# Re-dealing VectorE work and transposes between the attention and FFN stages of a fused transformer block

## The chip, the core and the metric

The kernel runs on one core of a Trainium2 chip. The metric is device microseconds of one execution. PE is TensorE, DVE is VectorE, ACT is ScalarE; SP issues the DMAs. PSUM is the memory into which the matmuls of this kernel write; a *bank* is one of the buffers in it that the kernel numbers 0 to 7. HBM is the memory outside the core.

Because the effect is below 1%, two measures are used. One is the time of whole runs. The other is read from each profile, and I call it **the stretch**: from the start of the first Q-projection matmul behind the first denominators (group 0 and 1) to the start of the first FFN matmul.

## The reference, cut to what matters

S = 2048 tokens, D = 1024, 32 heads of 32. With phi(t) = t+1 or exp(t), the linear attention is

```
q, k, v = split(layernorm_mod(x) @ wqkv)
pq, pk  = phi(q), phi(k)
kv      = sum over tokens of pk^T v          # per head, 32 x 32
den     = pq . sum(pk)                       # per token and head
x       = x + ga * ((pq @ kv / den) @ wo)
x       = x + gb * FFN(layernorm_mod(x))     # gelu(x@w_gate) * (x@w_up) @ w_down, F = 3584
```

## The kernel before, cut to what matters

The kernel never forms `pq @ kv`. It multiplies `kv` and `wo` first (W2 = kv @ wo, one product for each of 8 groups of 4 heads), scales pq by 1/den, and then multiplies pq by W2, one *output chunk* of 128 tokens at a time. "Q group" below means 512 tokens (4 chunks); there are four, numbered 0 to 3. Each group has 8 Q blocks of 128 columns.

1/den is made per head and token as a small row block, written to HBM and read back 32 times replicated ("rb" loads, 2 MB per Q group, in 8 DMAs), so that it lies on the same partitions as pq. Two rb buffers serve four groups, so the load for group 3 has to wait until the scaling of group 1 is done.

```
def phi(bank, dst, ...):                 # evacuates a Q block from PSUM
    ACT: EB = exp(PS(bank))
    DVE: EB = min(EB, 1) + 1e-6
    DVE: dst = max(PS(bank), 0) + EB     # now the bank is free

def pq_scale(sg, h, gs=((0, 2), (2, 4), (4, 6), (6, 8))):
    for g0, g1 in gs:                    # four DVE instructions, 128 x 512 each
        pq[sg][:, g0:g1, half h] *= RB[sg % 2][:, h, g0:g1]

def w2_pair(g):                          # PE: two matmuls into banks 2 and 3; ACT copies them to W2[g]

def q_next():                            # n counts the last 12 Q blocks, the last 8 are group 3; PSUM bank by turns
    b = (0, 1, 2, 0)[n] if n < 4 else (n + 1) % 2
    q_block(...); phi(b, ...)
# ... cut ...
q_next(); kvacc(15); zcols(); q_next(); den(0); rb_load(0); rb_load(1)
kvbd()                                   # DVE: masks kv out of PSUM, into kvbd
q_next(); q_next()
kvt()                                    # PE: 8 transposes of kvbd; ACT copies them
for u in range(8):                       # "W2 step": a Q block and a W2 product
    q_next()
    w2_pair(u)
    if u in (3, 5): pq_scale(0, (u - 3) // 2)
# ... cut ...
for c in range(12):                      # output chunks; banks 6,7 then 2,3 and 0,1 by turns
    wo_chunk(c)                          # 16 matmuls on PE, then DVE adds PSUM to x
    if c == 0: den(1); rb_load(2)
    if c in (0, 1): pq_scale(1, c)
    if c == 1: rb_load(3)
    if c in (4, 5, 6, 7): pq_scale(2 + (c - 4) // 2, c % 2)
    if c < 4: ln2_a(c)                   # layernorm on ACT, then a DMA transpose into h2
    if c == 9: mod2(0, 2); mod2(2, 2)    # 16 small DVE instructions on h2
# then FFN; chunks 12 to 15 are hooked into its first steps
```

## Time and profile before

| | before |
|---|---|
| time, median of the first 3 runs | 847.55 us (845.94 to 847.57) |
| span of the profiled run | 844.6 us |
| stretch | 67.58 us (179.80 to 247.38) |

The first part of the page gives the busy time of each engine, share of the span and number of instructions:

```profile
PE 835.1 (99%) x4229; PEld 386.9 (46%) x4229; DVE 491.8 (58%) x883; ACT 294.9 (35%) x483; POOL 24.3 (3%) x64
```

PE is the bound, so only a gap on PE is worth anything. The list of waits on PE (line, what it waited for, total us, times, longest) holds all of them:

```profile
PE ps_all L467 <- DMA c<-in_c_dram: 2.2, 1, 2.2
PE ps_all L928 <- DVE xall L935: 2.1, 2, 1.3
PE ps_all L565 <- DMA wmq<-in_w_mod_dram: 1.2, 1, 1.2
PE ps_all L653 <- DVE pq L604: 0.7, 1, 0.7
```

L467 and L565 belong to the start of the program. L928 is the matmul of an output chunk, L935 its add; L653 is the Q projection, L604 the last step of phi. The listed waits leave out the modelled tail of a matmul, about 0.16 us each. The loss is read better from the PE timeline (start, duration, line, count, idle before). A warm 512-column matmul takes 0.216 us from start to start:

```profile
179.80 3.63 PE L653 MATMUL ps_all<-h1T,wq 128*128 128x512 bf16 x16
183.35 1.07 PE L829 MATMUL ps_all<-ident,kvbd 128*128 128x128 bf16 x8
184.26 1.89 PE L653 MATMUL ps_all<-h1T,wq 128*128 128x512 bf16 x8
...
196.78 0.59 PE L837 MATMUL ps_all<-wo,kvt 128*128 128x512 bf16 x2
198.03 1.90 PE L653 MATMUL ps_all<-h1T,wq 128*128 128x512 bf16 x8 [0.65 <-DVE pq L604]
...
206.89 27.80 PE L928 MATMUL ps_all<-w,pq 128*128 128x512 bf16 x128
235.58 3.63 PE L928 MATMUL ps_all<-w,pq 128*128 128x512 bf16 x16 [0.89 <-DVE xall L935]
240.46 7.08 PE L928 MATMUL ps_all<-w,pq 128*128 128x512 bf16 x32 [1.26 <-DVE xall L935]
```

Four gaps: the 8 transposes (L829) take 0.91 us where 0.45 would do; the Q block at 198.03 could have started two matmuls after 196.78, at 197.21; the chunk at 235.58 could have started 128 matmuls after 206.89, at 234.51; the one at 240.46 at 239.03. The DVE timeline shows what stood in front of the instructions that PE waited for (L879 is the scaling, L604 frees a Q bank, L935 frees the banks of a chunk):

```profile
194.42 2.48 DVE L879 TENSOR_TENSOR pq<-pq,rb 128x512 bf16<-128x512 bf16 x4
...
197.28 0.69 DVE L604 SCALAR_TENSOR_TENSOR pq<-ps_all,eb 128x512 bf16<-128x512 f32 x1
...
231.89 2.50 DVE L879 TENSOR_TENSOR pq<-pq,rb 128x512 bf16<-128x512 bf16 x4 [2.35 <-DMA rb<-scr_rd]
234.30 1.22 DVE L935 TENSOR_TENSOR xall<-ps_all,xall 128x1024 bf16<-128x1024 f32 x1
236.78 2.50 DVE L879 TENSOR_TENSOR pq<-pq,rb 128x512 bf16<-128x512 bf16 x4 [1.25 <-DMA rb<-scr_rd]
239.19 2.34 DVE L935 TENSOR_TENSOR xall<-ps_all,xall 128x1024 bf16<-128x1024 f32 x2
```

At 194.42 a burst of four scalings stands before a phi. At 231.89 and 236.78 a burst first waits for its rb load to land and then runs, and the adds wait behind both.

### The profile page before, as it was taken

The page shows a single profiled execution, that of the slowest core. Times are in us where ns is not written, and L with a number is a line of the kernel's source. Part 1 is how long each engine was busy: PE and PEld are TensorE (multiplying, and loading weights), DVE is VectorE, ACT ScalarE, POOL GpSimd, SP SyncE. Part 2 cuts the span into 40 slices and gives each one's busy share as a digit, 9 for nine tenths or more (in the row PEclk, how much of TensorE's full clock was granted, in tenths as well). Part 3 has the DMA queues.
Part 4 walks back from the last instruction along what each step waited for, and adds up shares of the span by engine and source line. Part 5 has one row for each costly group of instructions (what it writes and reads, how often), then busy time and mean ns, then how long its engine had stood idle before and what let it go on. Part 6 is the DMA issues. An engine that isn't in the chain of part 4 may idle for free.

```text
span 844.6 us, 11333 instructions
## 1 busy us (share of the span) xinstructions
PE 835.1 (99%) x4229; PEld 386.9 (46%) x4229; DVE 491.8 (58%) x883; ACT 294.9 (35%) x483; POOL 24.3 (3%) x64
## 2 busy tenths in 40 slices
PE   8999999999989999999999999999999999999998
PEld 4454444444434444444444444444444444444445
DVE  5676767877775555564456665445556635565522
ACT  2343333345504345520344442034544204444300
POOL 2000000000200000010000001000000000000000
PEclk9999999999999999999999999999999999999999
DMA  9991824029957587341455533055553305555000
GB/s 283 355 284 26 262 53 98 14 59 238 197 119 222 157 264 205 100 107 31 126 156 154 156 107 81 26 155 151 150 150 100 75 19 156 151 153 145 7 19 26
DMA packets 181750, 112.70 MB, mean 133 GB/s; under 512 B 33080, under 2 KB 172728, under 8 KB 180672
## 3 DMA queue, kind: packets, MB, share of 16 engines
q1 hardware_dynamic: 181696, 111.98, 48.6%
q8 instruction: 34, 0.56, 0.3%
q14 instruction: 20, 0.16, 0.1%
HBM read 100.67 MB, written 4.47 MB: 124 GB/s over the span
## 4 chain that ended last, share of the span: by engine, by line
PE 92%; DMA 4%; SPq 2%; DVE 1%; issue 0%; ACT 0%; DVEq 0%; ACTq 0%
PE ps_all L1025 23%; PE ps_all L1000 23%; PE ps_all L997 23%; PE ps_all L612 12%; PE ps_all L653 6%; PE ps_all L928 3%; DMA rb<-scr_rd 1%; DMA wmq<-in_w_mod_dram 1%; DMA h2T<-xh 1%; PE ps_all L634 1%; DVE pq L879 1%; DMA scr_rd<-rdc 1%; SPq L443 0%; SPq L438 0%; PE ps_all L584 0%; SPq L868 0%
## 5 line engine op out<-in xcount | busy, mean ns | idle before, releaser
L997 PE MATMUL ps_all<-h2T,wg 128*128 128x512 bf16 x896 | 339.6, 379 | 0.0
L1000 PE MATMUL ps_all<-h2T,wu 128*128 128x512 bf16 x896 | 339.6, 379 | 0.0
L1025 PE MATMUL ps_all<-wd,yT 128*128 128x512 bf16 (+1 forms) x924 | 194.1, 373 | 0.0
L1008 ACT ACTIVATE q<-ps_all 128x512 f32<-128x512 f32 x112 | 66.9, 597 | 233.9 <-PE ps_all L997 233.9
L1025 PEld LDWEIGHTS ps_all<-wd,yT 128*128 128x128 bf16 x924 | 90.4, 98 | 103.3
L1000 PEld LDWEIGHTS ps_all<-h2T,wu 128*128 128x128 bf16 x896 | 87.7, 98 | 105.7
L997 PEld LDWEIGHTS ps_all<-h2T,wg 128*128 128x128 bf16 x896 | 87.7, 98 | 105.7
L1010 DVE SCALAR_TENSOR_TENSOR ww<-q,ps_all 128x512 f32<-128x512 f32 x112 | 77.0, 687 | 92.5 <-ACT guh L1009 92.5
L1013 DVE SCALAR_TENSOR_TENSOR ww<-th,guh 128x512 f32<-128x512 f32 x112 | 77.5, 692 | 77.9 <-ACT th L1012 77.9
L1012 ACT ACTIVATE th<-ww 128x512 f32<-128x512 f32 x112 | 70.5, 629 | 84.3 <-DVE ww L1010 84.3
L1015 DVE TENSOR_TENSOR yT<-ww,ps_all 128x512 bf16<-128x512 f32 x112 | 76.9, 687 | 3.8
L1030 DVE TENSOR_TENSOR ps_all<-ps_all,gbb 128x512 f32<-128x512 f32 (+1 forms) x33 | 22.5, 682 | 94.8 <-PE ps_all L1025 94.8
L1009 ACT ACTIVATE guh<-ps_all 128x512 f32<-128x512 f32 x112 | 66.3, 592 | 0.0
L601 ACT ACTIVATE eb<-ps_all 128x512 f32<-128x512 f32 x64 | 37.5, 601 | 78.5 <-PE ps_all L612 38.8
L653 PE MATMUL ps_all<-h1T,wq 128*128 128x512 bf16 x256 | 58.9, 379 | 0.7 <-DVE pq L604 0.7
L928 PE MATMUL ps_all<-w,pq 128*128 128x512 bf16 x256 | 56.6, 379 | 2.1 <-DVE xall L935 2.1
L612 PE MATMUL ps_all<-wk,h1T 128*128 128x512 bf16 x256 | 58.2, 379 | 0.0
L612 PE MATMUL ps_all<-wv,h1T 128*128 128x512 bf16 x256 | 57.7, 379 | 0.0
L602 DVE TENSOR_SCALAR eb<-eb 128x512 f32<-128x512 f32 x64 | 27.1, 424 | 34.6 <-ACT eb L601 34.2
L928 PEld LDWEIGHTS ps_all<-w,pq 128*128 128x128 bf16 x256 | 24.8, 98 | 32.8 <-DVE xall L935 3.1
L612 PEld LDWEIGHTS ps_all<-wv,h1T 128*128 128x128 bf16 x256 | 24.9, 98 | 29.8 <-DVE eb L602 0.3
L612 PEld LDWEIGHTS ps_all<-wk,h1T 128*128 128x128 bf16 x256 | 24.6, 98 | 29.6 <-DVE h1T L538 1.3
(81 smaller groups left out, 397.6 us busy)
## 6 DMA issues: line engine op xcount, KB each, us to landing
wg<-in_B_w_gate_dram SPq DMA_DIRECT2D x56, 512.0 KB, 3.9
wu<-in_B_w_up_dram SPq DMA_DIRECT2D x56, 512.0 KB, 5.1
wmst<-in_w_mod_dram SPq DMA_DIRECT2D x8, 1024.0 KB, 11.5
rb<-scr_rd SPq DMA_DIRECT2D x32, 256.0 KB, 9.0
wd<-in_B_w_down_dram SPq DMA_DIRECT2D x7, 1024.0 KB, 8.2
wmq<-in_w_mod_dram SPq DMA_DIRECT2D x8, 512.0 KB, 7.6
out_dram<-xall SPq DMA_DIRECT2D x31, 128.0 KB, 1.7
xall<-in_A_x_dram SPq DMA_DIRECT2D x3, 1024.0 KB, 11.7
```

The lines of the kernel that those rows point to most:

```text
L612: o = sch.op(T, lambda e, dc=dc: e.matmul(PS(bank), H1[sg][:, dc, ci * P:(ci + 1) * P], W_[:, dc, jg * 512:(jg + 1) * 512], start=(dc == 0 ...
L653: o = sch.op(T, lambda e, dc=dc: e.matmul(PS(b), WQ[:, dc, qc * P:(qc + 1) * P], H1[sg][:, dc, :], start=(dc == 0), stop=(dc == NDC - 1)), ...
L928: last[half] = sch.op(T, lambda e, g=g, half=half: e.matmul(PS(b0 + half), PQ[sg][:, g, ci * P:(ci + 1) * P], W2[:, g, half * 512:(half + ...
L997: og = sch.op(T, lambda e, dc=dc: e.matmul(PS(bg), WG[slot][:, dc, e_ * P:(e_ + 1) * P], H2[sg][:, dc, :], start=(dc == 0), stop=(dc == ND ...
L1000: ou = sch.op(T, lambda e, dc=dc: e.matmul(PS(bu), WU[slot][:, dc, e_ * P:(e_ + 1) * P], H2[sg][:, dc, :], start=(dc == 0), stop=(dc == ND ...
L1008: sch.op(A, lambda e: e.activation(Q1[j][:, :], PS(bg), ACTF.Square, scale=math.sqrt(GELU_A)), prd=pr(bg), wr=rq, note=f"q1 {fc}")
L1009: ogh = sch.op(A, lambda e: e.activation(GUH[j][:, :], PS(bg), ACTF.Copy, scale=0.5), prd=pr(bg), wr=rg, note=f"gh {fc}")
L1010: sch.op(V, lambda e: e.scalar_tensor_tensor(WW[j][:, :], Q1[j][:, :], 1.0, PS(bg), op0=ALU.add, op1=ALU.mult), rd=rq, prd=pr(bg), wr=rw, ...
L1012: sch.op(A, lambda e: e.activation(TH[j][:, :], WW[j][:, :], ACTF.Tanh, scale=GELU_C), rd=rw, wr=rt, note=f"th {fc}")
L1013: sch.op(V, lambda e: e.scalar_tensor_tensor(WW[j][:, :], TH[j][:, :], 1.0, GUH[j][:, :], op0=ALU.add, op1=ALU.mult), rd=rt + rg, wr=rw, n ...
L1015: sch.op(V, lambda e: e.tensor_tensor(YT[:, fc, :], WW[j][:, :], PS(bu), ALU.mult), rd=rw, prd=pr(bu), wr=r_yt(fc), note=f"yT {fc}")
L1025: o = sch.op(T, lambda e, b=b, fc=fc, c0=c0, c1=c1, n=n: e.matmul(PS(b, 0, n), YT[:, fc, ci * P:(ci + 1) * P], WDT[fc // 4][:, fc % 4, c0:c1],
```

## The change

Its intent: no burst of scalings in front of an instruction that frees PSUM, and no transposes before kvbd is done. Scalings of one Q group half come as two pieces of two instructions, one piece per step; those of group 3 move behind chunks 10 and 11 and the rest behind the last of them; the rb load of group 3 moves with them, behind the four DMA transposes on SP's queue; the KV transposes come one Q block later, so the W2 products lag one step, and the last one gets banks 4 and 5.

```
-        def w2_pair(g):
-            b0 = 2
+        def w2_pair(g, b0=2):
...
-        def pq_scale(sg, h, gs=((0, 2), (2, 4), (4, 6), (6, 8))):
+        GH = [((0, 2), (2, 4)), ((4, 6), (6, 8))]
+
+        def pq_scale(sg, h, gs):
...
-        kvt()
         for u in range(NG):
             q_next()
-            w2_pair(u)
-            if u in (3, 5):
-                pq_scale(0, (u - 3) // 2)
+            if u == 0:
+                kvt()
+            else:
+                w2_pair(u - 1)
+            if u in (2, 3):
+                pq_scale(0, 0, GH[u - 2])
+            if u in (5, 6):
+                pq_scale(0, 1, GH[u - 5])
+        w2_pair(NG - 1, 4)
...                                            # in the loop over chunks c_:
-            if c_ in (0, 1):
-                pq_scale(1, c_)
-            if c_ == 1:
+            if 1 <= c_ <= 8:
+                pq_scale(1 + (c_ - 1) // 4, (c_ - 1) // 2 % 2, GH[(c_ - 1) % 2])
+            if c_ == 4:
                 rb_load(3)
-            if c_ in (4, 5, 6, 7):
-                pq_scale(2 + (c_ - 4) // 2, c_ % 2)
+            if c_ in (10, 11):
+                pq_scale(3, 0, GH[c_ - 10])
...                                            # ahead of the FFN loop:
+        pq_scale(3, 1, GH[0] + GH[1])
```

## The prediction

> **What bounds the kernel.** TensorE. The page's first part has PE busy 835.1 of 844.6 us (99%), granted clock 1.0; the list of waits has four for PE, 6.2 us together, all before 241 us. Warm 512-column matmuls start 0.216 us apart, which agrees with the 215.7 ns of the Trainium skill, "TensorE: Matmul & The Clock Gate", section "Wait — 56ns, not 53.3ns?". From 247 us to the end the chain has no gap, so only gaps in 174 to 247 us, where the change acts, can be won back.
>
> **The gaps there** (PE timeline, start to start, less the matmuls at their pace):
> 1. KV transposes: 8 take 0.91 us where 8 x 0.057 = 0.45 would do; they wait for kvbd on DVE (182.80 to 184.08). Lost 0.46.
> 2. The last Q block starts at 198.03, not 197.21: its PSUM bank waits for the phi of block 5, which on DVE stands behind four scalings (194.42, 2.48 us). Lost 0.82.
> 3. Output chunk 9 starts at 235.58, not 234.50: its banks wait for chunk 7's residual add, behind four scalings that waited for an rb load of Q group 3 (231.89, after 2.35 us idle for DMA). Lost 1.08.
> 4. Chunk 10 starts at 240.46, not 239.03: the same with the last burst (236.78, after 1.25 us idle). Lost 1.43.
> Sum 3.79 us.
>
> **What the change removes, adds, moves.** No instruction is added or removed: the same matmuls, DMA bytes and 32 scalings of about 0.62 us. Bursts of 2.5 us become pieces of 1.25 us. A W2 step on DVE is then 1.1 (phi) + 1.25 = 2.35 us against PE's 2.16, but only in pairs of steps, and two Q banks give slack; a chunk is 1.22 + 1.25 = 2.5 against 3.45. VectorE being strict FIFO (same page, "Architectural detail"), place in its order decides what PE waits for. Transposes after the next Q block find kvbd done. The last W2 pair in other banks need not wait for a 1.0 us copy. The rb load for Q group 3 moves behind all four h2 transposes on the DMA queue: I estimate its halves land about 240 and 245 us, not 232 and 237, but its scalings now stand after chunks 10 and 11, and PE needs them only at chunk 12 (261 us before). The last transpose lands about 235, the h2 modulation runs about 238 to 242, and FFN can start at about 243.6.
>
> **On the critical path:** all four gaps are on PE's own chain. I expect 3.4 to 3.8 us back; perhaps 0.1 to 0.4 lost again at the start of FFN, where chunk 10's add (behind 16 modulations, 4.2 us) ends about when PE wants its bank.
>
> **Predicted:** 847.55 - 3.65 = 843.9 us; 842.3 to 845.9 holds it 8 times in 10 (the runs before spread 1.6 us). Faster by over 2%: 0.003; within 2%: 0.992; slower by over 2%: 0.005.
>
> **Right if the profile shows:** KV transposes in about 0.45 us; no PE wait on a phi at L653; none on the residual add in chunks 9 and 10; the first FFN matmul near 243.7 instead of 247.4, and all after it shifted alike; no DVE idle for rb loads before chunk 9; the last rb load landing later without PE waiting.
>
> **Wrong if:** the later rb load or the last h2 transpose holds DVE so long that the first FFN banks come late (new waits near 243 to 254 us); the W2 stage, now DVE-bound in places, makes Q blocks 6 or 7 wait; or noise hides 0.4%.

(In its point 2, "the last Q block" is a slip: the block at 198.03 is the last but one, and the phi it waits for is that of the block two before it.)

## More of the kernel before

The fourth part of the page, the chain of work that ended last, gives its shares by engine and already says that a DMA is part of it (by the page's list, about 1% each are the rb loads, the transposes into h2, the store of 1/den, and a weight load, wmq, at the start of the program):

```profile
PE 92%; DMA 4%; SPq 2%; DVE 1%; issue 0%; ACT 0%; DVEq 0%; ACTq 0%
```

## The result, and the profile after

| | before | after |
|---|---|---|
| time, median (lowest to highest), 4 runs each | 847.56 us (845.94 to 847.92) | 843.27 us (843.05 to 843.71) |
| span of the profiled run | 844.6 us | 841.3 us |
| stretch | 67.58 us | 64.54 us |

The ratio is 0.9954, 95% interval 0.9937 to 0.9971: a real gain of about 0.5%, inside the 2% that count as "same".

In the page of the kernel after, the first part and the shares of the chain by engine:

```profile
PE 830.7 (99%) x4149; PEld 387.9 (46%) x4229; DVE 492.0 (58%) x883; ACT 294.9 (35%) x483; POOL 24.4 (3%) x64
...
PE 96%; DVE 2%; issue 1%; ACT 1%; DMA 0%; ACTq 0%
```

The 4.4 us less of PE busy time must not be read as saved work. PE did the same 4229 matmuls (the weight loads are all there), but 80 records are missing, so busy time is missing with them. The run "only the chunk stage" below, which has all 4229 records, shows 835.0 us. The second line is a real difference as far as the rb loads, the h2 transposes and the store are gone from the chain; the weight load of the start is gone too, but that varies with the start (it is there again, at 1%, in that run below).

The waits on PE (line numbers moved: L928 became L934) and the PE timeline at the same places:

```profile
PE ps_all L467 <- DMA c<-in_c_dram: 2.2, 1, 2.2
PE ps_all L653 <- DVE pq L604: 0.7, 1, 0.7
PE ps_all L653 <- issue: 0.2, 1, 0.2
PE ps_all L653 <- DVE ve L483: 0.2, 1, 0.2
```

(The two waits of 0.2 us are as long as one matmul, and the run with all 4229 records does not list them; I take them for missing records.)

```profile
179.46 5.35 PE L653 MATMUL ps_all<-h1T,wq 128*128 128x512 bf16 x23
184.65 0.61 PE L829 MATMUL ps_all<-ident,kvbd 128*128 128x128 bf16 x8
185.92 1.90 PE L653 MATMUL ps_all<-h1T,wq 128*128 128x512 bf16 x8 [0.66 <-DVE pq L604]
...
206.00 38.16 PE L934 MATMUL ps_all<-w,pq 128*128 128x512 bf16 x172
244.00 0.38 PE L1003 MATMUL ps_all<-h2T,wg 128*128 128x512 bf16 x1
```

Eleven chunks (176 matmuls, 4 records missing) now run from 206.00 to 244.00 without a gap: 176 x 0.2158 = 37.98 us. The gaps in the chunk stage and before the last Q blocks are gone. On DVE the adds of the chunks now wait for PE and for no load; this is the one of chunk 7, for which chunk 9 waited before:

```profile
230.39 1.23 DVE L941 TENSOR_TENSOR xall<-ps_all,xall 128x1024 bf16<-128x1024 f32 x1 [1.03 <-PE ps_all L934]
```

But the KV transposes did not simply lose their wait. They now take their 0.45 us, and the Q block behind them starts at 185.92 instead of 184.65 + 0.45 = 185.10: a gap of 0.82 us that the kernel before did not have, in place of 0.46. The DVE timeline shows what that block waits for:

```profile
182.45 1.29 DVE L823 TENSOR_TENSOR kvbd<-ps_all,bmask 128x384 bf16<-128x384 f32 x3
...
184.72 0.42 DVE L602 TENSOR_SCALAR eb<-eb 128x512 f32<-128x512 f32 x1
185.17 0.69 DVE L604 SCALAR_TENSOR_TENSOR pq<-ps_all,eb 128x512 bf16<-128x512 f32 x1
```

The block needs bank 0. Its last user was the Q block two before it, whose phi stands on DVE behind kvbd and another phi, and ends at 185.86 (185.17 + 0.69).

The sum of the gaps explains the stretch: before, 0.46 + 0.82 + 1.07 + 1.43 = 3.78 us; after, 0.82. The difference, 2.96, is close to the 3.04 by which the stretch got shorter.

### The profile page after: what moved, and what is told of

Its sections match the earlier page's. It is cut to its first block, busy times and chain, and to the rows that moved or that the text cites. A ratio compares the mean times of both kernels' runs of the same rounds, so it can differ in the third digit from the quotient of the medians.

```text
span 841.3 us, 11255 instructions
## 1 busy us (share of the span) xinstructions
PE 830.7 (99%) x4149; PEld 387.9 (46%) x4229; DVE 492.0 (58%) x883; ACT 294.9 (35%) x483; POOL 24.4 (3%) x64
## 4 chain that ended last, share of the span: by engine, by line
PE 96%; DVE 2%; issue 1%; ACT 1%; DMA 0%; ACTq 0%
PE ps_all L1006 23%; PE ps_all L1031 23%; PE ps_all L1003 22%; PE ps_all L612 12%; PE ps_all L934 7%; PE ps_all L653 6%; PE ps_all L668 1%; PE ps_all L634 1%; DVE h1T L538 1%; PE ps_all L584 0%; PE ps_all L836 0%; PE ps_all L565 0%; PE ps_all L519 0%; DVE ww L1019 0%; DVE ww L1016 0%
## 5 line engine op out<-in xcount | busy, mean ns | idle before, releaser
L1003 PE MATMUL ps_all<-h2T,wg 128*128 128x512 bf16 x859 | 325.6, 379 | 0.0
L653 PE MATMUL ps_all<-h1T,wq 128*128 128x512 bf16 x245 | 56.8, 379 | 1.4 <-DVE pq L604 0.7
L934 PE MATMUL ps_all<-w,pq 128*128 128x512 bf16 x251 | 56.0, 379 | 0.3
L934 PEld LDWEIGHTS ps_all<-w,pq 128*128 128x128 bf16 x256 | 25.0, 98 | 30.2 <-issue 0.2
```

What stands on the lines that cost most here:

```text
L653: o = sch.op(T, lambda e, dc=dc: e.matmul(PS(b), WQ[:, dc, qc * P:(qc + 1) * P], H1[sg][:, dc, :], start=(dc == 0), stop=(dc == NDC - 1)), ...
L934: last[half] = sch.op(T, lambda e, g=g, half=half: e.matmul(PS(b0 + half), PQ[sg][:, g, ci * P:(ci + 1) * P], W2[:, g, half * 512:(half + ...
L1003: og = sch.op(T, lambda e, dc=dc: e.matmul(PS(bg), WG[slot][:, dc, e_ * P:(e_ + 1) * P], H2[sg][:, dc, :], start=(dc == 0), stop=(dc == ND ...
```

## The experiments

**Theory A.** In DVE's fixed order, an instruction that frees a PSUM bank waits for everything ahead of it. The two gaps of the chunk stage come from scalings that stand ahead of an add before their rb load has landed, and the time of the landing is set by the DMA queue, so time won earlier on PE is lost there again. The gain is therefore almost wholly from moving the scalings of group 3 behind the chunks.
**Rival B** (the sum in my prediction): the four gaps are independent and each is worth its length.
**Rivals E and F**: it is the smaller pieces that help; it is only the place of the scalings, and the order of the rb load and the DMA transposes is of no account.

The stretch was read in each profile:

| kernel | stretch, us | time, us (median) | before, same chip (median) |
|---|---|---|---|
| before / before, again | 67.58 / 67.96 | 847.18 (again) | 846.53 |
| after / after, again | 64.54 / 64.77 | 844.30 (again) | 846.54 |
| only the W2 stage dealt out | 68.52 | 846.80 | 846.53 |
| only the KV transposes moved | 67.74 | 846.99 | 846.53 |
| only the chunk stage dealt out | 65.09 | 843.67 | 846.53 |
| after, KV transposes as before | 64.26 | 843.20 | 846.54 |
| after, last W2 product in banks 2, 3 | 65.95 | 844.52 | 846.54 |
| after, whole bursts in the chunk stage | 64.54 | 843.26 | 846.81 |
| after, whole bursts in the W2 stage | 65.37 | 843.97 | 846.81 |
| after, group 1 scaled early, rb load of group 3 early | 64.54 | 842.90 | 846.81 |
| before, rb load of group 3 late | 78.29 | 856.76 (one run) | 846.81 |
| after, a third PSUM bank for Q blocks | 63.71 | 842.56 | 846.54 |

All gave the right result.

### One part of the change at a time

*Only the W2 stage*: the kernel before with

```
-            if u in (3, 5):
-                pq_scale(0, (u - 3) // 2)
+            if u in (2, 3):
+                pq_scale(0, 0, GH[u - 2])
+            if u in (5, 6):
+                pq_scale(0, 1, GH[u - 5])
```

> The kernel before with only the scaling of Q group 0 dealt in half-group pieces over four W2 steps. Theory A (the gaps of the chunk stage are pinned to the landing of the rb loads of Q group 3, which the DMA queue sets, so what PE wins earlier it waits for there): the 0.8 us wait of a Q block in the W2 stage goes, but chunk 9 and chunk 10 still start within about 0.3 us of where they start before (235.6 and 240.5), their two gaps grow by about 0.8 us together or chunk 9's alone, and the time is within 0.3 us of before. Rival B (the four gaps are independent and add): 0.8 us faster, about 846.7.

Its PE timeline:

```profile
196.51 0.59 PE L837 MATMUL ps_all<-wo,kvt 128*128 128x512 bf16 x2
196.94 1.89 PE L653 MATMUL ps_all<-h1T,wq 128*128 128x512 bf16 x8
...
205.79 28.08 PE L932 MATMUL ps_all<-w,pq 128*128 128x512 bf16 x128
236.23 3.63 PE L932 MATMUL ps_all<-w,pq 128*128 128x512 bf16 x16 [2.36 <-DVE xall L939]
241.12 7.08 PE L932 MATMUL ps_all<-w,pq 128*128 128x512 bf16 x32 [1.26 <-DVE xall L939]
```

The Q block no longer waits (196.94 is two matmuls behind 196.51), and the second denominators are done 1.1 us earlier than before. Yet chunk 9 starts at 236.23: its wait grew from 0.89 to 2.36 us and swallowed all. Rival B falls; the ratio is 1.0004 (0.9992 to 1.0017), and its 0.8 us would be 0.9991. The chunk starts were not within the 0.3 us that I had written, but 0.65 us later than in the first profile of the kernel before; they lie between the two profiles of that kernel (235.58 and 236.37 for chunk 9). Why the time won does not reach the rb load is seen in the chain of this kernel, where the row of 1/den goes to HBM, and the first rb load follows:

```profile
208.58 5.49 DMA scr_rd<-rdc
...
214.08 0.33 SPq L868
```

The same piece of the chain in the kernel before:

```profile
209.57 4.38 DMA scr_rd<-rdc
213.96 0.34 SPq L868
```

The store was issued 1 us earlier and landed at the same time. Ahead of it in the queue stand four weight loads of 512 KB. The Trainium skill, "DMA: Bandwidth & Descriptors", section "Queues, rings and completion order", says that each DMA engine consumes the descriptors of a ring in order; these two landings agree: the DMA engines were busy with the weight loads up to 212 us in both (DMA share 1.15 and 1.20 from 211 to 212, 0.23 and 0.48 from 212 to 213), and the store landed at 213.95 and 214.07. No run moved the weight loads, so this step rests on the traces alone.

*Only the KV transposes* (later by one Q block, W2 one step behind, last product in banks 4 and 5):

> The kernel before with only the KV transposes one Q block later, the W2 products one step behind and the last one in other banks. Theory A: the wait moves from the transposes to the next Q block and grows from about 0.46 to about 0.82 us, because that block's bank still holds the Q block whose phi stands behind the kvbd product on DVE; this loss of about 0.36 us is swallowed by the wait for the rb loads, so the time is within 0.3 us of before. Rival B (my prediction: the transposes' gap goes): 0.46 us faster.

The gap behind the transposes was 0.82 us and no wait was inside them; the stretch, 67.74, lies between those of the two profiles of before, and the ratio is 1.0005 (0.9992 to 1.0017). Rival B, which was my prediction for this part, falls by the trace; the whole runs alone would not exclude its 0.46 us (0.9995). That the loss of 0.36 us was swallowed later is not shown by this run: chunk 9's gap was 0.94 us, less than the 1.07 and 1.42 of the two profiles of before, but these two differ by as much.

*Only the chunk stage* (`GH` and the last two pieces of the diff above, on the kernel before):

> The kernel before with only the scaling of groups 1 to 3 re-dealt over the output chunks and the rb load of group 3 moved behind the transposes. Theory A: no PE wait on the residual add in chunks 9 and 10; the W2 stage keeps its waits of 0.46 and 0.82 us; time about 0.46 us above the kernel after, so about 843.7, 3 to 4 us faster than before: nearly all of the gain is here. Rival B (four gaps add): 2.5 us faster than before, about 845.0.

```profile
206.60 38.16 PE L930 MATMUL ps_all<-w,pq 128*128 128x512 bf16 x176
```

No wait in the chunks, and the 0.82 us of the Q block and the 0.46 of the transposes still there. The stretch is 2.5 us shorter than that of the first profile of before and 2.9 shorter than that of the second; ratio 0.9967 (0.9954 to 0.9979). The stretch of the first profile alone would fit rival B as well; it is the two runs above that decide. With this part alone about four fifths of the gain in the stretch is there (2.49 of 3.04 us), less than the "nearly all" that I had expected; with it in place the W2 part is worth its own 0.83 us (the run with whole bursts in the W2 stage, below), which it was not before.

*The kernel before, again*:

> The kernel before itself, profiled again, to see what varies from run to run. Theory A: the starts of chunks 9 and 10 vary by some tenths of a us with the landing of the rb loads (they were 235.58 and 240.46), and the sum of the two gaps with them, which would explain why its times spread 2 us and those of the kernel after 0.7 us. Rival: the chunk gaps are the same to 0.1 us and the spread comes from the start of the program, before 45 us.

Chunk 9 started at 236.37, not 235.58, and its gap was 1.42, not 1.07 us, while chunk 10's gap was 1.43 both times. The first Q block of the stretch was also 0.42 us later. Both theories hold in part: the start of the program varies, and the landing of the rb loads varies on top of it.

*The kernel after, again*:

> The kernel after itself, profiled again beside its variants. Theory A: gap of 0.82 us behind the KV transposes again, no gap in the chunks, time 843.0 to 843.8; its spread is below 1 us, as only the start of the program varies.

The stretch was 64.77 us with the same gap of 0.82 us, as expected. The 0.23 us above the first profile are two Q blocks that waited 0.1 us each (197.29 and 199.56): DVE had stood 0.41 us at the first scaling of group 0, whose rb load landed late, so the W2 stage has little slack even with the pieces. But the times were not as expected: 842.79 to 845.91 us. The view by windows of this run (stretch of time, length, PE, weight loads, DVE, ACT and POOL busy, granted clock, DMA share, GB/s) shows where:

```profile
20.00:24.00 4.00, 2.71 (x40) 1.60 (x39) 0.90 (x3) 0.00 (x0) 0.00 (x0) 0.93 0.98 305
24.00:28.00 4.00, 4.00 (x18) 1.55 (x17) 0.00 (x0) 0.00 (x0) 0.00 (x0) 0.64 1.01 323
```

In the profiled run the granted clock fell to 0.64 at 24 to 28 us, long before any changed line, and the stretch began at 182.08 instead of 179.46. The longest wait on PE's list there is 1.24 us, at 22.10; what lowered the clock is not shown. That is why I rest small differences on the stretch and not on medians.

### Does size or place count?

*Whole bursts in the chunk stage, at the late places*: the kernel after with

```
-            if 1 <= c_ <= 8:
-                pq_scale(1 + (c_ - 1) // 4, (c_ - 1) // 2 % 2, GH[(c_ - 1) % 2])
+            if c_ in (2, 4, 6, 8):
+                pq_scale(1 + (c_ - 2) // 4, (c_ - 2) // 2 % 2, GH[0] + GH[1])
...
-            if c_ in (10, 11):
-                pq_scale(3, 0, GH[c_ - 10])
+            if c_ == 11:
+                pq_scale(3, 0, GH[0] + GH[1])
```

> The kernel after with the scalings of groups 1 to 3 whole again (bursts of four, 2.5 us), but at its late places: behind chunks 2, 4, 6, 8 and 11. Theory A (in the chunk stage place counts, not size: a burst of 2.5 us and an add of 1.2 us stay below the two chunks, 6.9 us, after which PE wants the banks again): no wait in the chunks, the stretch from the Q block behind the first denominators to the first FFN matmul stays at 64.5 to 64.8 us as in the kernel after. Rival E (it is the pieces that help): waits on the residual add come back, 1 us or more.

The stretch is 64.54 us, as in the kernel after, and no chunk waits. In the chunk stage the pieces bought nothing; the place did. Rival E falls there.

*Whole bursts in the W2 stage*: the kernel after with `if u in (2, 5): pq_scale(0, (u - 2) // 3, GH[0] + GH[1])`.

> The kernel after with the scaling of group 0 whole again, in two bursts of four behind W2 steps 2 and 5. Theory A (in the W2 stage size counts: a burst of 2.5 us and a phi of 1.1 us pass the 2 steps of 2.16 us after which PE wants the Q bank again, less the time the block itself takes): one Q block waits about 0.8 us behind the first burst; the second burst costs nothing, as no later block wants that bank; stretch 0.7 to 0.9 us longer than after. Rival: only the distance between the bursts mattered, stretch as after.

```profile
194.07 0.59 PE L836 MATMUL ps_all<-wo,kvt 128*128 128x512 bf16 x2
195.32 1.90 PE L653 MATMUL ps_all<-h1T,wq 128*128 128x512 bf16 x8 [0.65 <-DVE pq L604]
```

The first burst made one Q block wait 0.82 us (195.32 less 194.07 less two matmuls), the second none; the stretch is 65.37, 0.83 more than after. In the W2 stage size counts: two banks serve the Q blocks, so PE wants a bank again after two steps of 2.16 us, of which the block itself takes 1.73; a burst of 2.49 and a phi of 1.1 us do not fit in the 2.6 us that are left.

### The order of the loads

*Group 1 scaled early and the rb load of group 3 ahead of three of the transposes again; group 3 still scaled late*: the kernel after with

```
+            if c_ in (0, 1):
+                pq_scale(1, c_, GH[0] + GH[1])
+            if c_ == 1:
                 rb_load(3)
+            if 5 <= c_ <= 8:
+                pq_scale(2, (c_ - 5) // 2, GH[(c_ - 5) % 2])
```

in place of the lines for chunks 1 to 8.

> The kernel after with the scaling of group 1 back behind chunks 0 and 1, so that the rb load of group 3 can again stand ahead of three of the four h2 transposes on the DMA queue; group 3 is still scaled behind chunks 10 and 11. Theory A: no wait in chunks 9 and 10, but the last transpose lands about 240 us instead of 235, so the h2 modulation on DVE starts 1 to 3 us later than 238.4 and the first FFN matmul waits for it or for the adds behind it: stretch 1 to 3 us longer than the 64.5 us of after. Rival F (only the place of the scalings counts, the order of the loads is of no account): stretch as after.

My theory missed here and rival F was right: the stretch is 64.54 us. The DVE timeline tells why:

```profile
238.37 1.23 DVE L941 TENSOR_TENSOR xall<-ps_all,xall 128x1024 bf16<-128x1024 f32 x1 [1.03 <-PE ps_all L934]
239.51 4.19 DVE L538 TENSOR_SCALAR h2T<-h2T,cb1T,sbT 128x256 bf16<-128x256 bf16 x16
```

The h2 modulation (L538) starts right behind the add. Its first 8 instructions need the first two transposes only, the last 8 the other two, so the last transposes had half of the 4.19 us, 2.1 us, more than I gave them, and no wait of DVE shows. So the later rb load is a consequence of when group 1 frees the buffer, and neither helps nor hurts by itself.

*The reverse, the rb load late but the scalings of group 3 where they were*: the kernel before with `rb_load(3)` behind chunk 4 instead of chunk 1.

> The kernel before with the rb load of group 3 behind the transposes but its scalings still behind chunks 6 and 7. Theory A: DVE stands at the first of these scalings until the load lands, near 240 us, with the adds of chunks 7 and 8 behind it: chunk 9 starts near 244 instead of 235.6, and the stretch grows by 6 to 10 us over the 67.6 us of before. Rival F: about as before.

Its DVE timeline, and then its windows:

```profile
240.75 2.50 DVE L879 TENSOR_TENSOR pq<-pq,rb 128x512 bf16<-128x512 bf16 x4 [11.31 <-DMA rb<-scr_rd]
243.17 1.22 DVE L935 TENSOR_TENSOR xall<-ps_all,xall 128x1024 bf16<-128x1024 f32 x1
```

```profile
234.00:240.00 6.00, 0.32 (x2) 0.00 (x0) 0.00 (x0) 0.00 (x0) 0.00 (x0) 0.73 1.05 233
...
246.00:248.00 2.00, 2.00 (x6) 0.76 (x5) 2.00 (x5) 0.00 (x0) 0.00 (x0) 0.50 1.17 285
```

DVE stood 11.31 us at the first scaling, chunk 9 started at 244.44, and the stretch grew by 10.7 us to 78.29, a little more than I had allowed. One thing that I had left out: PE idled long enough that its clock was halved (0.50 in the windows from 240 to 250 us) and the chunks behind the wait ran slowly. The Trainium skill, "TensorE: Matmul & The Clock Gate", section "What's actually happening", gives half the clock after an idle window of about 3.4 us; this run agrees on the half, but the clock fell sooner, 2.2 to 2.7 us after PE's last matmul had ended at 234.32 (1.00 up to 236.5, 0.50 from 237). The slow clock explains why my estimate was passed: the last three chunks took 13.44 us where 48 matmuls at pace take 10.5, 2.9 of the 10.7 us. (One run only.) Together the two runs say: moving the load late without its scalings costs over 10 us, so rival F does not hold there; moving the scalings late without the load loses nothing of the gain.

### What each of the small parts is worth

*After, with the KV transposes and W2 products where they were*:

> The kernel after without the move of the KV transposes and the W2 products (both kinds of scaling re-dealt, transposes and banks as before). Theory A: the gap of 0.82 us behind the transposes is 0.46 us again, inside them; no other gap from 180 to 262 us; time 0.3 to 0.4 us below the kernel after: this part of the change costs. Rival D (the move is what the prediction took it for): 0.46 us above the kernel after.

The gap was 0.46 us again, inside the transposes, and the stretch 64.26, 0.28 us below the first profile of after and 0.51 below the second: this part of the change costs. In whole runs the difference is not clear of noise (0.9959, 0.9945 to 0.9973, against 0.9969, 0.9954 to 0.9985, for the kernel after on the same chip).

*After, with the last W2 product in banks 2 and 3*:

> The kernel after with the last W2 product in the banks of the others. Theory A: it has to wait for the copy of the product before it, which ended about 202.3 us where the product stood at 201.0: PE loses about 1.2 us there, and the time is about 1.2 us above the kernel after. Rival: the wait hides behind the first output chunk, same time as after.

```profile
201.00 0.59 PE L836 MATMUL ps_all<-wo,kvt 128*128 128x512 bf16 x2
202.83 0.60 PE L836 MATMUL ps_all<-wo,kvt 128*128 128x512 bf16 x2 [1.23 <-ACT w L838]
```

PE waits for ACT's copy of the product before; 202.83 less 201.00 less two matmuls is 1.40 us, and the stretch is 1.41 above after. The other banks are needed because the lagging W2 leaves two products in a row at the end.

*After, with a third PSUM bank for the Q blocks*:

```
-            b = (0, 1, 2, 0)[qn[0]] if qn[0] < 4 else (qn[0] + 1) % 2
+            b = (0, 1, 2, 0, 1, 5, 0, 1, 5, 0, 1, 0)[qn[0]]
```

> The kernel after with one more PSUM bank in the rotation of the last Q blocks (bank 5, free once kvbd has been read from it), so that the block behind the KV transposes does not reuse the bank of a block whose phi is still queued behind kvbd on DVE. Theory A (with the chunk stage freed, PE is bound by nothing but its own work, and a gap taken away shows in the time): the 0.82 us gap goes, no wait of PE is left between 180 and 262 us, the first FFN matmul starts 0.8 us earlier relative to the first KV product, time about 0.8 us below the kernel after, near 842.5. Rival C (the new wait is swallowed downstream, as the early gaps of the kernel before were): same time as after.

```profile
185.43 0.61 PE L829 MATMUL ps_all<-ident,kvbd 128*128 128x128 bf16 x8
185.88 1.89 PE L653 MATMUL ps_all<-h1T,wq 128*128 128x512 bf16 x8
...
205.96 38.16 PE L934 MATMUL ps_all<-w,pq 128*128 128x512 bf16 x172
```

The Q block starts 0.45 us behind the transposes: no gap is left in the stretch, which is 63.71 us, 0.83 less than after. The time is 842.56 us, ratio to before 0.9948 (0.9937 to 0.9959); it is the best kernel, by a margin over after that the profile shows and that whole runs alone would not (after had 843.27 in its first runs and 844.30, disturbed by the clock at the start, beside this one).

## Why the prediction was right, and where it was not

- **Total**: 843.9 us predicted, 843.27 measured, "same" predicted and measured. That these are so close is partly luck: the stretch gave 3.04 us (2.81 to 3.42 over the pairs of profiles) and not the 3.4 to 3.8 expected; the rest of the 4.29 us between the medians is not in the stretch. The bound (PE, its own gaps only) and the size (under 0.5%) were right, because PE's gaps in the stretch are an upper limit to what a re-ordering can win, and nothing behind the stretch waits for anything (597.26 us in both kernels).
- **Gaps 3 and 4 (chunks 9 and 10)**: predicted to go, went. The first FFN matmul came at 244.00 for a predicted 243.6 to 243.7, helped by a stretch that began 0.34 us earlier than before (179.46, not 179.80).
- **Gap 2 (Q block behind the burst)**: predicted to go, went, and the whole-burst run gives 0.83 us for it.
- **Gap 1 (KV transposes)**: wrong. I wrote "Transposes after the next Q block find kvbd done", which is true, and left out that the next Q block then needs a bank whose phi queues behind the same kvbd. The gap became 0.82 instead of 0.46 us: a loss of 0.36 where I had booked a gain of 0.46. My own test "no PE wait on a phi at L653" failed with it (0.66 us at 185.92).
- **Loss at the start of FFN** (0.1 to 0.4): none was seen. Chunks and FFN follow each other at pace.
- **The sum of four gaps**: near for the change as a whole (3.65 us booked, 3.04 found in the stretch; gap 1 left 0.82), but wrong as a way of costing its parts. The W2 gap alone was worth nothing (ratio 1.0004), as the rb landing downstream absorbs it; only once that is off the chain do the others count.
- **rb load of group 3 behind the transposes**: I estimated landings of about 240 and 245 us. In the run with the late load, DVE's waits for it end at 240.75 and, for the second half, at 245.43. I had given the earlier transposes a share in the early start of FFN; the run with the early load shows that they had none.

What stays open: the medians of the first runs differ by 4.29 us, the profiled stretches by 3.04 (3.42 against the second profile of before). The start of the program and the landing of the rb loads vary by some tenths each between the two profiles of before; I have no profile of each timed run to show that they make up the rest.

## What to carry to other kernels

When PE is 99% busy, list its gaps, and for each one ask which instruction frees what PE waits for and what stands ahead of that on its in-order engine; work whose data comes by DMA belongs behind such an instruction, not in front, as long as its own consumer is far. Do not add up gaps that lie on one chain: a gap whose end is set by a DMA landing can absorb what is won before it (here 0.82 us), so remove that one first. When work is delayed until its input is ready, check the bank or buffer that the next instruction reuses, since the wait may only move there, and grow.

## What the Trainium skill lacked or had wrong

- "Perfetto Trace Analysis": I found no word there that a profile can lack matmul records. Here 80 of 4229 are missing in the kernel after and none in the kernel before, which looks like 4.4 us less PE busy time. It is not the code: the kernel before with the load of group 3 late lacks 80 too, and the kernel with only the chunk stage changed lacks none.
- "DMA: Bandwidth & Descriptors": it has no rate for loads that replicate one row of HBM over 32 partitions. While only rb loads ran (192 to 196 us of the kernel before) they moved 217 GB/s at a DMA share of 0.99, against 371 GB/s at a share of 1.06 for the input loads at 40 to 44 us. The rb loads are 256 KB each and those issued at 40 to 44 us 1024 KB, so what of this is size and what is the replication is not separated.
- "TensorE: Matmul & The Clock Gate": half the clock after an idle window of about 3.4 us was not exact here: in the run with the late load it fell 2.2 to 2.7 us after the last matmul's end.
- Nothing else in the pages used was contradicted: 0.216 us per 512-column matmul, and waits that fit in-order engines and rings, were seen.
